# Third half of the attention: its queries and keys turned by DMA transposes in place of TensorE, weight loads put in another order, and one exponential placed later

## The chip, the cores and the metric

The kernel runs on one core of one Trainium2 chip. The metric is the device time of the whole kernel in microseconds; the time before is 238.54 us, the median of three runs (237.76 to 238.59). The trace is of one further execution, with a span of 236.1 us.

## The reference

An attention with a sliding window and a few global keys is followed by a feed-forward network with a ReLU gate. The attention takes 4 sequences of 768 positions, 8 heads of 64; each query sees 8 global keys and the last 96 keys, with a slope per head on the distance:

```python
keep = is_global | is_local
dist = np.where(is_global & ~is_local, float(n_local), np.abs(rel).astype(np.float32))
scores = scale * np.matmul(q, k.transpose(0, 1, 3, 2)) - slopes[:, None, None] * dist[None, :, :]
scores = np.where(keep, scores, -1000000000.0)
a = softmax(scores)
x = np.matmul(a, v)                     # -> 3072 tokens x 512
out = (np.maximum(x @ w_gate, 0.0) * (x @ w_val)) @ w_out   # 512 -> 1536 -> 512
```

## The kernel before

**Tiles and stages.** The 3072 tokens are cut into eight *halves* s = 0 to 7 of 384 query positions (half a sequence, all 8 heads). A half passes through three steps: queries and keys are loaded, cast to bf16 and transposed (features on partitions); attention gives xT, the transposed input of the feed-forward network; and the network gives 384 rows of output. Heads go in four pairs p = 0 to 3.

**Feed-forward.** For each of 12 chunks of the inner dimension there are two *items*, a gate and a value product, each of four matmuls of 128 x 384 (L745) and some 0.65 us. ScalarE takes the ReLU of the gate (L754) and VectorE multiplies it by the value product (L761). The output product works on pairs of 128 tokens and saves multiplications by sums of blocks: sums of w_out (`weight_sums`, L597, eight VectorE subtractions, once in the kernel: four matrices T, each in two parts for the two halves of the chunks), sums of the hidden values (L624 to L627), and seven products p1 to p7 (L631) whose partial results are copied by ScalarE (L660) and added by VectorE (L644). The weights come in three groups of four chunks (`wg[i]`, `wv[i]`), w_out in one tile `wo_sb`.

**Attention.** `attention_pieces(s)` is a list of 30 entries: units of scores (L512: matmuls into PSUM banks, of which one comes from `av_psum`, two banks, and the others from `qk_psum`, three banks), exponentials on ScalarE (L521), masks on VectorE (L533), value products `piece_av(s, p, e)` (L431, one for each head e of pair p, each in an `av_psum` bank), whose last lines are a logarithm of the row sums on ScalarE (L440) and, for the second head of the pair, exp(-log) (L445, the inverse), and `piece_norm` (L450), the products on VectorE of the value product and the inverse, which write xT and free the bank.

**What sets the order.** Everything is written out in one order, by `weave`: items of the feed-forward network of half c come one after the other, and pieces with a position between 0 and 1 are put in as soon as that share of the feed-forward work is done. `spread(items, first, last)` gives the i-th of n pieces the position first + (i + 0.5)/n times the stretch. The engines take their instructions in this order; an instruction whose input isn't ready holds up what is behind it on its engine. In the loop at L995 (c = 2 to 7) attention of half c + 1 lies beside the network of half c (`spread` from 0 to 0.87 for an even c, 0.85 for an odd one). The networks of halves 0 and 1 are woven together in two weaves (L985, L991), the first over weight groups 0 and 1, the second over group 2 and the output products, with attention of half 2 beside it.

**Transposes.** From half 3 on, `early_pieces(s)` does them: casts on GpSimd (L366), three transposing transfers for the keys and three for the queries, issued by SyncE (L371), and, again on GpSimd, copies that put the keys in order (L374). Half 2 does it in another way: GpSimd casts into `obuf` (L258 and L975), TensorE transposes by 24 small matmuls (L299, called by `T2_piece`), VectorE copies the keys (L278 to L280) and ScalarE the queries (L982).

**Loads.** GpSimd issues most transfers of this phase one after the other on one queue: weight groups 1 and 2 (L173), keys and queries of half 2 (L113), w_out (L923) and, after the casts of half 2, the values of half 2 (L162).

Of the kernel before, what the change touches and what calls it, by code (L numbers as in the profile page):

```python
# [8 lines left out]
FP32 = mybir.dt.float32  # L9
BF16 = mybir.dt.bfloat16  # L10
FP16 = mybir.dt.float16
AF = mybir.ActivationFunctionType
# [4 lines left out]
def kernel(  # L17
# [12 lines left out]
    nc = tc.nc  # L30
# [4 lines left out]
    DM = H * D  # L35
    DFF = moe_w_gate.shape[1]
    N_DC = DM // 128
    N_FC = DFF // 128
    HP = H // 2
    QH = S // 2  # L40
# [6 lines left out]
    scale = 1.0 / math.sqrt(D)  # L47
# [7 lines left out]
    for half in range(2):  # L55
# [14 lines left out]
    rc_pool = ctx.enter_context(tc.tile_pool(name="rc", bufs=2))  # L70
    xt_pool = ctx.enter_context(tc.tile_pool(name="xt", bufs=3))
# [19 lines left out]
    qT2 = [qTb[1].rearrange("d p e t -> d (p e t)")[:, i * HP * QH : (i + 1) * HP * QH].rearrange(  # L91
        "d (p t) -> d p t", p=HP) for i in range(2)]
# [9 lines left out]
    wo_sb = const.tile([128, N_FC, DM], FP16)  # L102
# [59 lines left out]
    def load_v_half(s):  # L162
        b, half = divmod(s, 2)
        if half == 0:
            load_v_globals(b)
            spread_v_globals(b)
        for j in range(4) if half == 0 else range(4, NT):
            load_v(b, j)

    def load_w(dst, src, f0, f1):  # L170
        nc.gpsimd.dma_start(out=dst, in_=src[:, f0:f1].rearrange("(c p) f -> p c f", p=128))  # L171

    def load_w_group(i):  # L173
        load_w(wg[i], moe_w_gate, i * GW * 128, (i + 1) * GW * 128)
        load_w(wv[i], moe_w_val, i * GW * 128, (i + 1) * GW * 128)

    for p in range(HP):
        load_qk(0, 2 * p, 2 * p + 2)
# [72 lines left out]
    QKB, FFB, AVB = (qk_psum, "qk_ps"), (ff_psum, "ff_ps"), (av_psum, "av_ps")  # L251
    xT_of = {}
# [35 lines left out]
    def piece_t(s, p, pool=av_psum, name="av_ps", apart=False):  # L288
        for i in (1, 0):
            if i == 1 or apart:  # L290
                tp = pool.tile([128, 512], FP32, name=name)
                tp = tp[:, 0:QH].bitcast(BF16).rearrange("d (i t) -> d i t", i=2)
            tp_of[s, p, i] = tp[:, i, :]
            for n in range(NN):
                for e in range(2 if s == 1 else 1):
                    r = slice(64 * e, 64 * e + 64) if s == 1 else slice(0, 128)
                    src = (qk16[s, i][:, 2 * p + e, n * D : (n + 1) * D] if s == 1
                           else cast_of[s, p][:, i, n])
                    nc.tensor.matmul(tp[r, i, n * 128 : (n + 1) * 128],  # L299
                                     lhsT=src, rhs=ident, is_transpose=True,  # L300
                                     start=((i == 1 or apart) and n == 0),
                                     stop=((i == 0 or apart) and n == NN - 1))

    def piece_copy_k(s, p):
        b, half = divmod(s, 2)
        put_keys(nc.vector.tensor_copy, nc.vector.tensor_copy, kT[b % 2][p], tp_of[s, p, 1], half)
# [71 lines left out]
    def early_pieces(s):  # L378
        out = [(0.0, lambda p=p: piece_cast2(s, p, kc, ks_of)) for p in range(HP)]
        out += [(0.0, lambda n=n: piece_x(kNb[s % 2], kc[s % 2], n)) for n in range(NN)]  # L380
        out += [(0.0, lambda p=p: piece_cast2(s, p, qc, qs_of)) for p in range(HP)]
        out += [(0.0, lambda n=n: piece_x(qT2[s % 2], qc[s % 2], n)) for n in range(NN)]
        out += [(0.0, lambda p=p: piece_order(s, p)) for p in range(HP)]
        return out
# [35 lines left out]
    def piece_av(s, p, e):  # L420
        b, half = divmod(s, 2)
        h = 2 * p + e
        vb = vbuf[b % 2]
        av = av_psum.tile([128, 512], FP32, name="av_ps")
        av_of[s, p, e] = av
        av3 = av[:, 0:QH].rearrange("d (n p) -> d n p", n=NN)
        todo = [t for bank in banks_of_half[half] for t in bank]
        for i, (j, a, w, m) in enumerate(todo):
            es, c = es_of[s, p, j, e]
            z0 = 2 * D * h + (D if e == 0 else 0)  # L430
            nc.tensor.matmul(av3[:, :, a : a + w],  # L431
                             lhsT=vb[:, j, z0 : z0 + 128],
                             rhs=es[:, c : c + NN * w].rearrange("k (n p) -> k n p", n=NN),
                             start=(i == 0), stop=(i == len(todo) - 1),
                             skip_group_check=True)
        o0, d0 = (0, 64) if e == 0 else (64, 0)
        if e == 0:
            av_of[s, p, "l"] = rc_pool.tile([128, QH], FP32, name="lnd")
        ln = av_of[s, p, "l"]
        nc.scalar.activation(ln[o0 : o0 + 64], av[d0 : d0 + 64, 0:QH], AF.Ln, bias=0.0, scale=1.0)  # L440
        if e == 1:
            if s not in xT_of:
                xT_of[s] = xt_pool.tile([128, N_DC, QH], BF16, name="xT")
            rc = rc_pool.tile([128, QH], FP32, name="rcp")
            nc.scalar.activation(rc, ln, AF.Exp, bias=0.0, scale=-1.0)  # L445
            av_of[s, p, "r"] = rc

    def piece_norm(s, p, e):
        r = slice(64 * e, 64 * e + 64)
        nc.vector.tensor_tensor(xT_of[s][r, p, :], av_of[s, p, e][r, 0:QH], av_of[s, p, "r"][r],  # L450
                                op=ALU.mult)
# [88 lines left out]
    def attention_pieces(s):  # L540
        masks, units = [], []

        def flush():
            for f in masks:
                f()
            masks.clear()

        def scores(groups, pools):
            units.extend(score_unit(s, groups, list(pools)))

        def x(scored=None):
            ready = masks[:]
            masks.clear()
            if scored:
                scores(*scored)
            masks.append(unit_exp(s, *units.pop(0)))
            for f in ready:
                f()

        U = [([(0, 0), (0, 1)], (AVB, QKB, QKB, QKB)),  # L560
             ([(0, 2), (1, 0)], (AVB, QKB, QKB, QKB)),
             ([(1, 1), (1, 2)], (AVB, QKB, QKB, QKB))]
        X = lambda u=None: [(0.0, lambda: x(u))]
        AV = lambda p: [(0.0, lambda e=e: (flush(), piece_av(s, p, e))) for e in range(2)]
        N = lambda p: [(0.0, lambda: (piece_norm(s, p, 0), piece_norm(s, p, 1)))]
        wait = [(0.0, lambda: None)]
        a0, a1 = AV(0), AV(1)

        return (X(U[0]) + X() + X() + X() + wait + X(U[1]) + X() + X() + a0[0:1] + X() + a0[1:2] + N(0) + wait
                + X(U[2]) + X() + a1[0:1] + X() + X() + a1[1:2] + N(1) + wait * 2 + AV(2) + N(2) + wait * 2  # L570
                + AV(3) + N(3))


    out_v = out.rearrange("(s p n) d -> s n p d", p=128, n=NN)
# [17 lines left out]
    def weight_sums(i0, i1):  # L592
        b = lambda f, d: B(i0, i1, f, d)
        t = lambda n: T(n, i0, i1)
        for out_, x, y in ((t(1), b(0, 1), b(0, 0)), (t(2), b(1, 1), t(1)),
                           (t(4), b(1, 0), t(2)), (t(3), b(1, 1), b(0, 1))):
            yield lambda o=out_, x=x, y=y: nc.vector.tensor_tensor(o, x, y, op=ALU.subtract)  # L597
# [207 lines left out]
    def spread(items, first, last):  # L805

        n = len(items)
        return [(first + (i + 0.5) / n * (last - first), f) for i, (_, f) in enumerate(items)]
# [14 lines left out]
    def cast(s, p, ek, eq):  # L823
        piece_cast(s, p, 1, ek)
        piece_cast(s, p, 0, eq)
# [11 lines left out]
    def AV(s, p, *pools):  # L837
        piece_av_wide(s, p, *pools)
        piece_norm_wide(s, p)
# [78 lines left out]
    piece_biased(1, 0)  # L918
    load_v(0, 3, 24)
    load_w_group(1)  # L920
    load_w_group(2)
    load_qk(2, 0, H, nc.gpsimd)
    load_w(wo_sb, moe_w_out, 0, DM)  # L923
    for f in gate[0:3]:
        f(0, LAST)
    for f in gate[0:3]:
# [45 lines left out]
    nc.gpsimd.memset(vbuf[1][:, NT - 1, :].bitcast(mybir.dt.uint32), 0)  # L972
    for j in range(NT):
        fill_ones(nc.gpsimd, 1, j)
    for p in range(HP):  # L975
        cast(2, p, P, P)
    load_v_half(2)

    def T2_piece(p):
        piece_t(2, p, *QKB, apart=True)  # L980
        piece_copy_k(2, p)
        nc.scalar.copy(qT2[0][:, p], tp_of[2, p, 0])  # L982

    T2 = [(0.0, lambda p=p: T2_piece(p)) for p in range(HP)]
    weave(f1_1[G[0]] + f1_0[G[1]][4:] + f1_1[G[1]],  # L985
          [(0.05 + 0.06 * j, lambda j=j: fill_ones(nc.vector, 0, j)) for j in range(NT)],
          [(0.1 + 0.2 * i, lambda h=h: setup_mask(h)) for i, h in enumerate((0, 1, 6, 7))],
          [(0.6, lambda: load_qk(3, 0, H)), (0.6, lambda: load_v_half(3))],
          spread(T2, 0.55, 0.95))
    sums_wo = [(0.0, f) for i in (0, 3) for f in weight_sums(i, i + 3)]  # L990
    weave(f1_0[G[2]] + f1_1[G[2]] + f2_0 + f2_1,  # L991
          spread(attention_pieces(2), 0.02, 0.86), spread(early_pieces(3), 0.1, 0.76),
          spread(sums_wo, 0.08, 0.4))

    for c in range(2, NHALF):  # L995
        placed = []
# [43 lines left out]
```

The softmax here doesn't subtract the row's maximum and nothing guards it: scores larger than these inputs give would overflow.

## Time and profile before

| | |
|---|---|
| time, median of 3 | 238.54 us (237.76 to 238.59) |
| span of the trace | 236.1 us |
| TensorE busy | 228.7 us, 97% of the span |
| VectorE busy | 186.9 us, 79% |
| ScalarE busy | 146.2 us, 62% |
| GpSimd busy | 89.0 us, 38% |
| moved by DMA | 30.43 MB, mean 129 GB/s |

The busy share of an engine is a mean over stages with different limits. The chain of waits goes back from the last instruction and says for each moment who held up the end: TensorE has 83% of it. The slices are 40 equal parts of the span, each digit a busy share in tenths. In the timelines a row gives start, duration, engine, line and what is done; what stands in brackets is the idle time before it and what ended that.

### The profile page before, as it was taken

What the parts mean: (1) busy time and instruction counts of PE and PEld (TensorE: products, weight loads), DVE (VectorE), ACT (ScalarE), POOL (GpSimd) and SP (SyncE); (2) the same over time, 40 slices, a digit from 0 to 9 for tenths busy, and PEclk for the clock granted to TensorE, in tenths of its full rate; (3) what the DMA queues carried; (4) which work ended last, traced back from release to release, by engine and by line L of the source; (5) the groups of instructions that cost most, each with busy time, mean ns of one, the idle gap of its engine ahead of it and who ended that gap; (6) DMA issues with size and microseconds to landing.
All of it is one profiled execution on the core that took longest, in us unless ns stands there. A gap on an engine that the chain in (4) does not pass through costs nothing.

```text
span 236.1 us, 5512 instructions
## 1 busy us (share of the span) xinstructions
PE 228.7 (97%) x2021; PEld 157.7 (67%) x2021; DVE 186.9 (79%) x466; ACT 146.2 (62%) x321; POOL 89.0 (38%) x191
## 2 busy tenths in 40 slices
PE   7898999999999999999999999999999999999994
PEld 3674766656678666856688566856688566865683
DVE  6876867879988779886999779876899779863784
ACT  7988865667624887467842787557742687624310
POOL 8997913933483066406580066405340000000000
PEclk9999999999999999999999999999999999999999
DMA  5999999998459856856397764846412200020005
GB/s 167 203 168 183 206 262 282 171 118 267 72 155 170 250 149 106 52 176 204 90 81 119 236 175 90 53 143 214 93 44 89 92 0 3 0 92 0 1 3 178
DMA packets 71419, 30.43 MB, mean 129 GB/s; under 512 B 47744, under 2 KB 70784, under 8 KB 71392
## 3 DMA queue, kind: packets, MB, share of 16 engines
q0 software_dynamic: 34896, 10.27, 38.7%
q1 hardware_dynamic: 36496, 19.82, 29.7%
q8 instruction: 16, 0.26, 0.5%
q14 instruction: 11, 0.09, 0.1%
HBM read 28.38 MB, written 6.29 MB: 147 GB/s over the span
## 4 chain that ended last, share of the span: by engine, by line
PE 83%; DVE 5%; POOL 4%; DMA 4%; ACT 2%; issue 1%; POOLq 0%; DVEq 0%
PE ff_ps L745 49%; PE ff_ps L631 19%; PE av_ps L431 6%; DMA kc<-in_q_dram 4%; PE ff_ps L778 2%; PE av_ps L512 2%; PE qk_ps L512 2%; POOL vbuf L154 1%; DVE wo_sum L597 1%; DVE obuf L644 1%; DVE ht L761 1%; DVE es L533 1%; POOL kc L131 1%; PE av_ps L465 1%; POOL wg L171 1%
## 5 line engine op out<-in xcount | busy, mean ns | idle before, releaser
L754 ACT ACTIVATE grelu<-ff_ps 128x384 bf16<-128x384 f32 x96 | 46.8, 489 | 52.6 <-PE ff_ps L745 39.3
L745 PE MATMUL ff_ps<-xT,wg 128*128 128x384 bf16 x384 | 77.9, 326 | 0.2 <-DMA wg<-in_moe_w_gate_dram 0.2
L745 PE MATMUL ff_ps<-xT,wv 128*128 128x384 bf16 x384 | 77.9, 326 | 0.0
L761 DVE TENSOR_TENSOR ht<-ff_ps,grelu 128x384 f16<-128x384 f32 x96 | 53.4, 557 | 27.6 <-PE ff_ps L745 23.5
L745 PEld LDWEIGHTS <-wv 128*128 128x128 bf16 x384 | 36.0, 98 | 23.9 <-issue 1.1
L745 PEld LDWEIGHTS <-wg 128*128 128x128 bf16 x384 | 36.3, 97 | 21.7 <-issue 0.7
L450 DVE TENSOR_TENSOR xT<-av_ps,rcp 64x384 bf16<-64x384 f32 x48 | 26.6, 553 | 6.1 <-ACT rcp L445 5.3
L367 POOL CAST kc<-ks 128x384 bf16<-128x384 f32 x20 | 10.6, 569 | 54.5 <-DMA ks<-in_k_dram 54.5
L644 DVE TENSOR_TENSOR obuf<-ff_ps,obuf 128x512 f32<-128x512 f32 (+1 forms) x46 | 27.6, 604 | 3.6 <-PE ff_ps L631 0.9
L440 ACT ACTIVATE lnd<-av_ps 64x384 f32<-64x384 f32 x48 | 23.3, 485 | 11.1 <-PE av_ps L431 10.2
L533 DVE TENSOR_TENSOR es<-es,m_all 128x432 bf16<-128x432 bf16 (+3 forms) x108 | 29.9, 321 | 0.2 <-ACT es L521 0.2
L521 ACT ACTIVATE es<-qk_ps 128x432 bf16<-128x432 f32 (+2 forms) x54 | 27.6, 531 | 0.0
L154 POOL DMA_DIRECT2D vbuf<-in_v_dram x29 | 24.7, 860 | 0.1
L431 PEld LDWEIGHTS <-vbuf 128*128 128x128 bf16 x216 | 18.2, 98 | 4.8 <-DVE xT L450 0.4
L431 PE MATMUL av_ps<-es,vbuf 128*128 128x216 bf16 (+4 forms) x216 | 21.4, 226 | 0.0
L631 PEld LDWEIGHTS <-ht 128*128 128x128 f16 x198 | 18.6, 97 | 3.5 <-issue 0.8
L631 PEld LDWEIGHTS <-hsum 128*128 128x128 f16 x192 | 18.5, 98 | 2.1
L631 PE MATMUL ff_ps<-wo_sb,ht 128*128 128x256 f16 x132 | 18.3, 272 | 0.0
L631 PE MATMUL ff_ps<-wo_sum,hsum 128*128 128x256 f16 x144 | 17.2, 272 | 0.0
L445 ACT ACTIVATE rcp<-lnd 128x384 f32<-128x384 f32 x24 | 12.6, 523 | 0.8
L521 ACT ACTIVATE es<-av_ps 128x432 bf16<-128x432 f32 (+2 forms) x18 | 9.5, 527 | 2.0 <-PE qk_ps L512 2.0
L512 PEld LDWEIGHTS <-kT 64*128 64x128 bf16 x216 | 6.6, 94 | 6.1 <-issue 3.8
(130 smaller groups left out, 263.6 us busy)
## 6 DMA issues: line engine op xcount, KB each, us to landing
out_dram<-obuf SPq DMA_DIRECT2D x22, 256.0 KB
ks<-in_k_dram SPq DMA_DIRECT2D x5, 768.0 KB
qs<-in_q_dram SPq DMA_DIRECT2D x5, 768.0 KB
vbuf<-in_v_dram POOLq DMA_DIRECT2D x23, 120.0 KB, 4.7
wv<-in_moe_w_val_dram POOLq DMA_DIRECT2D x3, 512.0 KB, 10.5
wo_sb<-in_moe_w_out_dram POOLq DMA_DIRECT2D x1, 1536.0 KB, 21.0
wg<-in_moe_w_gate_dram POOLq DMA_DIRECT2D x2, 512.0 KB, 10.3
ks<-in_k_dram SPq DMA_DIRECT2D x4, 192.0 KB
```

The source lines that it names most:

```text
L154: nc.gpsimd.dma_start(out=v_dst(b, NG + r0, NG + r0 + n, j), in_=v[b, :, KT * j + r0 : KT * j + r0 + n, :].rearrange("h p d -> p h d"))
L431: nc.tensor.matmul(av3[:, :, a : a + w], lhsT=vb[:, j, z0 : z0 + 128], rhs=es[:, c : c + NN * w].rearrange("k (n p) -> k n p", n=NN), star ...
L440: nc.scalar.activation(ln[o0 : o0 + 64], av[d0 : d0 + 64, 0:QH], AF.Ln, bias=0.0, scale=1.0)
L450: nc.vector.tensor_tensor(xT_of[s][r, p, :], av_of[s, p, e][r, 0:QH], av_of[s, p, "r"][r], op=ALU.mult)
L512: nc.tensor.matmul(banks[e][:, c : c + NN * w], lhsT=kT[b % 2][p][r, j, :], rhs=q3[:, :, a : a + w], start=True, stop=True)
L521: nc.scalar.activation(es[:, 0:cols], ps[:, 0:cols], AF.Exp, bias=0.0, scale=scale)
L533: nc.vector.tensor_mul(e4, e4, mk)
L631: nc.tensor.matmul(ps[:, c0 : c0 + DH], lhsT=lhs(i), rhs=rhs(i), start=(i == 0), stop=(i == NP - 1), skip_group_check=True)
L644: add = lambda o, x, y: nc.vector.tensor_tensor(o, x, y, op=ALU.add)
L745: nc.tensor.matmul(st[key][:, 0:QH], lhsT=w_of(w, dc, fc), rhs=xT_of[c][:, dc, :], start=(dc == 0), stop=(dc == N_DC - 1))
L754: nc.scalar.activation(gr, psg[:, 0:QH], AF.Relu, bias=0.0, scale=1.0)
L761: nc.vector.tensor_tensor(ht[:, fc, :], psv[:, 0:QH], st["r", fc], op=ALU.mult)
```

## The change

The keys and queries of half 2 are transposed as those of the later halves are, by `early_pieces(2)`, so that TensorE, VectorE and ScalarE have no part in it. The transfers are re-ordered for it: keys and queries of half 2 come before weight group 2, which GpSimd now issues behind its casts of half 2; w_out comes in two loads, one ahead of these casts and one behind. The copies that order the keys follow the loads of the values on GpSimd. With VectorE free of the key copies, half of the sums of w_out goes into the first weave (positions 0.6 to 0.95), the other half stays in the second (0.2 to 0.4); attention of half 2 is placed from 0.09 to 0.9 in place of 0.02 to 0.86. Last, the inverse of pair 3 is a piece of its own after the value product of its second head, in all halves from 2 on; the list has 31 entries by that.

```diff
+    def load_wo(i):
+        f = N_FC // 2
+        nc.gpsimd.dma_start(out=wo_sb[:, i * f : (i + 1) * f], in_=moe_w_out[
+            i * f * 128 : (i + 1) * f * 128].rearrange("(c p) f -> p c f", p=128))
...
-        if e == 1:
-            if s not in xT_of:
-                xT_of[s] = xt_pool.tile([128, N_DC, QH], BF16, name="xT")
-            rc = rc_pool.tile([128, QH], FP32, name="rcp")
-            nc.scalar.activation(rc, ln, AF.Exp, bias=0.0, scale=-1.0)
-            av_of[s, p, "r"] = rc
+        if e == 1 and p < HP - 1:
+            piece_inverse(s, p)
+
+    def piece_inverse(s, p):
+        rc = rc_pool.tile([128, QH], FP32, name="rcp")
+        nc.scalar.activation(rc, av_of[s, p, "l"], AF.Exp, bias=0.0, scale=-1.0)
+        av_of[s, p, "r"] = rc
...
-                + AV(3) + N(3))
+                + AV(3) + [(0.0, lambda: piece_inverse(s, 3))] + N(3))
...
     load_w_group(1)
-    load_w_group(2)
     load_qk(2, 0, H, nc.gpsimd)
-    load_w(wo_sb, moe_w_out, 0, DM)
+    load_wo(0)
...
-    for p in range(HP):
-        cast(2, p, P, P)
+    early = early_pieces(2)
+    for _, f in early[:-HP]:
+        f()
+    load_w_group(2)
+    load_wo(1)
     load_v_half(2)
...
-    T2 = [(0.0, lambda p=p: T2_piece(p)) for p in range(HP)]
+    for _, f in early[-HP:]:
+        f()
+
+    sums_wo = [[(0.0, f) for f in weight_sums(i, i + 3)] for i in (0, 3)]
...
-          spread(T2, 0.55, 0.95))
-    sums_wo = [(0.0, f) for i in (0, 3) for f in weight_sums(i, i + 3)]
+          spread(sums_wo[0], 0.6, 0.95))
     weave(f1_0[G[2]] + f1_1[G[2]] + f2_0 + f2_1,
-          spread(attention_pieces(2), 0.02, 0.86), spread(early_pieces(3), 0.1, 0.76),
-          spread(sums_wo, 0.08, 0.4))
+          spread(attention_pieces(2), 0.09, 0.9), spread(early_pieces(3), 0.1, 0.76),
+          spread(sums_wo[1], 0.2, 0.4))
```

More of the change, by code (lines that the diff above doesn't have):

```diff
@@ L440, in piece_av @@
         nc.scalar.activation(ln[o0 : o0 + 64], av[d0 : d0 + 64, 0:QH], AF.Ln, bias=0.0, scale=1.0)
-        if e == 1:
-            if s not in xT_of:
-                xT_of[s] = xt_pool.tile([128, N_DC, QH], BF16, name="xT")
-            rc = rc_pool.tile([128, QH], FP32, name="rcp")
-            nc.scalar.activation(rc, ln, AF.Exp, bias=0.0, scale=-1.0)
-            av_of[s, p, "r"] = rc
+        if e == 1 and p < HP - 1:
[4 more added lines that the diff above has]
+        av_of[s, p, "r"] = rc
     def piece_norm(s, p, e):
+        if s not in xT_of:
+            xT_of[s] = xt_pool.tile([128, N_DC, QH], BF16, name="xT")
         r = slice(64 * e, 64 * e + 64)
@@ L974 @@
         fill_ones(nc.gpsimd, 1, j)
-    for p in range(HP):
-        cast(2, p, P, P)
-    load_v_half(2)
[L979 to L982, printed above, removed]
-    T2 = [(0.0, lambda p=p: T2_piece(p)) for p in range(HP)]
+    early = early_pieces(2)
[3 more added lines that the diff above has]
+    load_wo(1)
+    load_v_half(2)
+    for _, f in early[-HP:]:
+        f()
+    sums_wo = [[(0.0, f) for f in weight_sums(i, i + 3)] for i in (0, 3)]
     weave(f1_1[G[0]] + f1_0[G[1]][4:] + f1_1[G[1]],
```

## The prediction

> **What bounds the kernel now.** I read the first page's busy times, the slices over the span, the chain of waits, then the timelines of the stages that the edits touch.
>
> ```profile
> PE 228.7 (97%) x2021; PEld 157.7 (67%) x2021; DVE 186.9 (79%) x466; ACT 146.2 (62%) x321; POOL 89.0 (38%) x191
> PE   7898999999999999999999999999999999999994
> DVE  6876867879988779886999779876899779863784
> DMA  5999999998459856856397764846412200020005
> PE 83%; DVE 5%; POOL 4%; DMA 4%; ACT 2%; issue 1%; POOLq 0%; DVEq 0%
> ```
>
> TensorE is busy from about 25 us to the end and is 83% of the chain, so work taken off it counts fully, and any wait put in front of it counts too. DMA is full up to 53 us. The chain shows where something else holds TensorE: VectorE around 50 to 59 us, and later ScalarE for a moment.
>
> ```profile
> 40.54 0.34 PE qk_ps L299 x6
> 42.17 0.34 PE qk_ps L299 x6
> 58.81 0.47 DVE xT L450
> 59.33 0.26 PE av_ps L512
> 124.69 0.49 ACT lnd L440
> 125.20 0.52 ACT rcp L445
> 125.73 0.27 ACT obuf L660
> 126.04 1.03 PE ff_ps L631 x8
> ```
>
> (Columns: start, duration, what.) The L299 groups are the third half's transposes. At 59.33 a score group waited for an attention output (L450). At 126.04 a product waited for a ScalarE copy (L660) that stood behind a logarithm and an exponential.
>
> ```profile
> 50.00:55.00 5.00, 5.00 (x43) 2.96 (x42) 4.63 (x13) 3.91 (x10) 0.00 (x0) 1.00 1.15 117
> 55.00:60.00 5.00, 4.85 (x41) 2.96 (x40) 4.94 (x12) 3.58 (x9) 2.97 (x5) 1.00 0.76 259
> 83.00:88.00 5.00, 5.00 (x47) 3.13 (x46) 3.74 (x10) 4.14 (x10) 3.83 (x8) 1.00 0.48 139
> ```
>
> (Stretch and length; busy time of TensorE, its weight loads, VectorE, ScalarE, GpSimd; clock; DMA share; GB/s.) VectorE is full from 50 to 60 us, where the eight weight sums (L597, 0.3 to 0.85 us each) lie. At 83 to 88 us, a steady stage, it is not.
>
> **What the Trainium skill says.** "TensorE: Matmul & The Clock Gate", section "Wait — 56ns, not 53.3ns?": a warm matmul follows the last after its columns at 2.4 GHz and about 2.5 ns; 24 transposes of 128 columns are then 24 x 55.8 = 1.34 us, and the trace agrees (four groups at 0.34). "DMA: Bandwidth & Descriptors", section "Queues, rings and completion order": a DMA engine serves the queues that have work in turn, packet by packet. So transposes and weight loads in flight together share the engines; before, the two never met while TensorE waited, so no run here shows it.
>
> **The change, part by part.**
>
> *Transposes.* Four TensorE groups go: 4 x 0.34 = **-1.34 us**, on the path. Twelve VectorE key copies (L278 to L280, 1.1 us for each pair of heads) go from 40 to 47 us, and four ScalarE copies (L982, 0.48 us); nobody waited for these there, so they count nothing.
>
> *Weight sums.* Half of the eight go to the time that the key copies leave free. VectorE is relieved by about 2 us between 50 and 59, and the wait at 59.33 (TensorE idle 58.85 to 59.33 of which 0.15 is the gap of any score group) goes: **-0.25 us** (estimate 0.2 to 0.4).
>
> *Loads.* Now keys and queries of the third half follow the second weight group, at the pitch of the landings in the trace: wv1 at 35.7 stood behind wg2, which in turn moves. In place of ks landing 37.65 and qs 39.62, ks lands near 32.5 and qs near 34.5, and the first half of wo near 38.3. GpSimd (waiting 7.48 us for ks before the cast at 37.70, see below) starts the casts at 32.6; eight at about 0.46 us and the wait for qs end at 36.4. Only then do the issues of wg2, wv2 and wo's second half come, 0.8 us each; then the values' loads. Uncontended, at 2.55 us for each half megabyte, wg2 lands near 40.9, wv2 43.4, the second wo 47.2, the values' globals 47.4. The deadlines: gate 8 reads wg2 at 46.91 now, at 45.6 with the transposes gone; val 8 reads wv2 at 46.2; the second sums read wo at about 52; the values are read at 54.6. There are 4.7 and 2.8 us of slack.
>
> ```profile
> 37.70 0.50 POOL L263 CAST obuf<-ks 128x384 bf16<-128x384 f32 x1 [7.48 <-DMA ks<-in_k_dram]
> 59.65 3.92 SPq L372 DMA_TRANSPOSE kN<-kc  x3
> ```
>
> Against this stand the six DMA transposes, from 34.5 to 42.3 by the pitch of the next half (3.92 us for three), in the same stretch. How much of the engines they take there is not shown. Lower bound 0 (the engines fit them between the packets of the loads). Upper bound: a burst of all engines of 0.65 us each, as the next half's seem to be, all pushed in front: 6 x 0.65 = 3.9 us, wg2 at 44.8, wv2 at 47.3, i.e. a wait of 47.3 - 46.2 = 1.1 us, and later values another 0.4. I take 0, because the slack covers 2.8 of the 3.9 us. The key copies on GpSimd now stand behind the value loads' issues (43 to 47.4); the first scores at 48.3 - 1.3 = 47.0 want the first pair at about 44. Small risk, 0.
>
> *The last exponential.* Its inverse of pair 3 becomes an item of its own behind the second value product. In stages c=3 and c=5 the copy L660 is then ahead of it: the waits at 126.04 (0.23) and 179.75 (0.23) go: **-0.46 us**. An attention output at 146.28 (0.17) profits too: **-0.17 us**.
>
> But the list of attention pieces has 31 in place of 30 items, and `spread` gives position (i+0.5)/31 of the same stretch: *all* pieces of all later stages move forward by up to 3%, that is by none or one feed-forward item of 0.65 us. In stages c=2, 4 and 6 the order of instructions changes from [value product, 2 items, value product, 3 items, scores, 1 item] to [.., 2 items, .., 2 items, scores, 2 items]: the third score unit comes one item earlier.
>
> ```profile
> 83.90 0.47 PE L431 MATMUL av_ps<-es,vbuf 128*128 128x72 bf16 x5
> 84.21 0.81 PE L745 MATMUL ff_ps<-xT,wg 128*128 128x384 bf16 x4
> 84.85 0.81 PE L745 MATMUL ff_ps<-xT,wv 128*128 128x384 bf16 x4
> 85.50 0.81 PE L745 MATMUL ff_ps<-xT,wg 128*128 128x384 bf16 x4
> 86.25 0.25 PE L512 MATMUL av_ps<-qT,kT 64*128 64x192 bf16 x1
> ...
> 85.50 1.14 DVE L450 TENSOR_TENSOR xT<-av_ps,rcp 64x384 bf16<-64x384 f32 x2
> ```
>
> (The last line is VectorE's timeline.) The unit at 86.25 needs an av_ps bank of two; it is freed by the first of the two products L450, 85.50 to 86.07. That one waits for logarithm and exponential (84.42 to 85.46) of the value product at 83.90, which doesn't move. One item earlier the unit would start at 85.6 and cannot before 86.2: TensorE idles about **0.5 us**, and the feed-forward item that hid it now comes after. The products L450 of pair 2 similarly: the first value product of pair 3 (95.79) moves one item forward to 95.14, but its bank is freed by a product that stands behind a ReGLU product and a sum on VectorE until 94.75, so it ends at 95.4 or so: **0.38 us**. The pair before: 0.12 us. Together 1.0 us a stage, three stages: **+3.0 us**. Bounds: 0.4 a stage if only the first is real and partly covered, 1.2 if the delays push ScalarE and VectorE work behind. I take 1.0. In stages c=3 and 5, I find value products an item earlier and no bank missing: 0.
>
> *Placement 0.09 to 0.9.* In the second weave the attention starts 7% of the stretch later; it gives the loads some slack and is otherwise neutral: 0.
>
> Sum: -1.34 - 0.25 - 0.46 - 0.17 + 3.0 = **+0.8 us**; 238.54 + 0.8 = 239.3.
>
> **Rivals.**
> *A, the moved items find room.* The stalls of the even stages are half as long, because a wait early in the stage makes the later ones shorter (TensorE's wait at the third unit also gives VectorE time for pair 2). Then +1.0 instead of +3.0: 238.5 - 1.2 = 237.3; with 0 it is 236.3. For it: VectorE has idle gaps around 84 and 88. Against: both waits are chains of fixed length from a value product that moves with TensorE. 0.27.
> *B, the loads are late (slower).* The transposes displace the weights fully: +1.1 for wv2, +0.4 for the values, on top of the main case: 240.8. For it: the DMA share of the slices is 9 until 53 us, and wg2 is issued 14 us later than now. Against: 2.8 us slack. 0.22.
> *C, stalls gone and loads late:* about 238.5. 0.06.
>
> **How the numbers follow.** Main case 0.45 at 239.3 (238.5 to 240.2, about a third of it above 239.73), A 0.27 at 237.0 (236.3 to 237.8, two thirds below 237.35), B 0.22 at 240.8, C 0.06. Faster by over 0.5% (below 237.35): from A, 0.2. Slower (above 239.73): 0.15 of the main case and all of B, 0.37. The rest, 0.43, within 0.5%. The range takes in A's middle and most of B: 236.8 to 241.2.
>
> **What would show it.** After: no L299 groups between 40 and 46; no wait of the gate and value products of weight group 2 (L745's idle column for a weight load stays near 0.2); the score group near 59 without a VectorE wait; in the three even stages, gaps of about 0.5 us before the third score unit that the chain gives to the attention output product; none before product p4 at 126 and 180. If the even stages keep their length, A is right. If TensorE idles at 45 to 48 us for a weight, B is. The prediction is wrong if the stalls shift other engines' queues into a better order, which static positions don't show.

## The result and the profile after

The changed kernel takes 248.34 us (median of 6 runs, 247.36 to 249.12) where the kernel before takes 237.95 us (236.97 to 238.59): a ratio of 1.044, 95% interval 1.040 to 1.048. Forecast were 239.3 us and a range of 236.8 to 241.2. The line numbers below are those of each kernel's own text; in the changed one the items are L753 (before L745), the scores L520 (L512), the value products L436 (L431), `piece_norm` L458 (L450), and the transposes L377 (L372). Where executions of one kernel lie more than 1.5% apart, as with x7 and x12 below, the ratio is taken from the faster ones.

The first page of the changed kernel, the lines that answer to those shown of before:

```profile
PE 231.2 (94%) x1997; PEld 157.8 (64%) x1997; DVE 187.6 (76%) x454; ACT 145.5 (59%) x317; POOL 94.8 (38%) x204
PE   5889999939899999999999999999999999999994
DVE  5688867614999778977799877977799876964684
PEclk9799999967999999999999999999999999999999
DMA  6999999999329893369439584568330400020004
PE 69%; DMA 12%; DVE 9%; ACT 5%; SPq 1%; issue 1%; POOL 0%; DVEq 0%; ACTq 0%
```

TensorE has a hole in the ninth slice (49 to 55 us) that was not there, and in it and behind it the clock is at 6 and 7 tenths. Of the chain of waits DMA now has 12%, against 4%. Half of that is the first load of w_out, on the chain from 24.6 to 38.5 us, where TensorE was busy all the time; the rest is what it waited for:

```profile
38.91 1.30 SPq L377
40.25 1.33 SPq L377
41.63 11.82 DMA qT<-qc
53.59 0.34 PE av_ps L520
54.10 0.39 PE qk_ps L520 x5
54.49 5.30 PE ff_ps L753 x20
```

The last query transpose was issued at 41.63 and had landed at 53.45; the first scores of half 2 waited for it, with TensorE idle for 4.08 us. The stretches around it, in the columns used before (TensorE, its weight loads, VectorE, ScalarE, GpSimd, clock, DMA share, GB/s):

```profile
49.00:51.00 2.00, 0.51 (x4) 0.10 (x1) 0.56 (x1) 0.39 (x1) 2.00 (x6) 1.00 1.35 179
51.00:53.00 2.00, 0.00 (x0) 0.00 (x0) 0.00 (x0) 0.00 (x0) 1.27 (x2) 0.64 1.97 149
55.00:57.00 2.00, 2.00 (x8) 0.95 (x7) 0.09 (x1) 1.08 (x3) 0.00 (x0) 0.50 2.30 150
57.00:59.00 2.00, 2.00 (x10) 1.04 (x9) 1.14 (x3) 0.78 (x3) 0.00 (x0) 0.65 0.89 179
```

From 49.5 to 53.6 TensorE has nothing; from 51.6 to 58.4 its clock is half, and from 54.4 to 58.2 the matmuls of an item start 0.32 us apart in place of 0.16.

Where the 10 us arose is seen best by setting the start of the same feed-forward item in two traces side by side. There are 192 items, 24 for each half; the number is what the difference to the trace of before grew by in the stretch:

| stretch | after | 31 pieces, rest as before (x2) |
|---|---|---|
| up to item 8 (start of the kernel) | +1.3 | -0.8 |
| items 8 to 32 (both groups, transposes of half 2 among them) | -1.4 | +0.9 |
| items 32 to 40 (first scores of half 2) | +5.9 | 0.0 |
| item 40 to the start of c=2 (rest of the second weave) | +1.7 | -0.2 |
| c=2 | +1.25 | +1.5 |
| c=3 | -0.3 | -0.3 |
| c=4 | +1.0 | +1.0 |
| c=5 | -0.3 | -0.2 |
| c=6 | +1.0 | +1.0 |
| sum | +10.1 | +2.9 |

The start of the kernel is the same code in all and differs by -0.8 to +1.3 among the profiled executions (a first load of queries that lands a us sooner or later); I count it as no effect. What x2 gained there it gave back by item 24, in a wait.

### The profile page after: what moved, and what is told of

Its sections match the earlier page's. It is cut to its first block, busy times and chain, and to the rows that moved or that the text cites. A ratio compares the mean times of both kernels' runs of the same rounds, so it can differ in the third digit from the quotient of the medians.

```text
span 246.4 us, 5459 instructions
## 1 busy us (share of the span) xinstructions
PE 231.2 (94%) x1997; PEld 157.8 (64%) x1997; DVE 187.6 (76%) x454; ACT 145.5 (59%) x317; POOL 94.8 (38%) x204
## 3 DMA queue, kind: packets, MB, share of 16 engines
q0 software_dynamic: 34912, 10.27, 38.1%
## 4 chain that ended last, share of the span: by engine, by line
PE 69%; DMA 12%; DVE 9%; ACT 5%; SPq 1%; issue 1%; POOL 0%; DVEq 0%; ACTq 0%
PE ff_ps L753 37%; PE ff_ps L639 19%; DMA wo_sb<-in_moe_w_out_dram 6%; PE av_ps L436 5%; DMA qT<-qc 5%; PE av_ps L520 2%; PE ff_ps L786 2%; DVE ht L769 2%; PE qk_ps L520 2%; DMA qs<-in_q_dram 2%; DVE xT L458 1%; SPq L377 1%; ACT grelu L762 1%; DVE obuf L652 1%; DVE es L541 1%
## 5 line engine op out<-in xcount | busy, mean ns | idle before, releaser
L762 ACT ACTIVATE grelu<-ff_ps 128x384 bf16<-128x384 f32 x96 | 46.8, 491 | 56.3 <-PE ff_ps L753 40.0
L753 PE MATMUL ff_ps<-xT,wg 128*128 128x384 bf16 x384 | 79.1, 330 | 0.2
L753 PE MATMUL ff_ps<-xT,wv 128*128 128x384 bf16 x384 | 78.6, 328 | 0.0
L753 PEld LDWEIGHTS <-wg 128*128 128x128 bf16 x384 | 37.0, 98 | 23.8 <-issue 2.9
L753 PEld LDWEIGHTS <-wv 128*128 128x128 bf16 x384 | 36.3, 98 | 23.8 <-issue 1.7
L541 DVE TENSOR_TENSOR es<-es,m_all 128x432 bf16<-128x432 bf16 (+3 forms) x108 | 33.5, 354 | 4.5 <-ACT es L529 4.5
L372 POOL CAST kc<-ks 128x384 bf16<-128x384 f32 x24 | 12.7, 573 | 62.6 <-DMA ks<-in_k_dram 62.6
L458 DVE TENSOR_TENSOR xT<-av_ps,rcp 64x384 bf16<-64x384 f32 x48 | 26.6, 554 | 5.7 <-ACT rcp L451 4.8
L436 PEld LDWEIGHTS <-vbuf 128*128 128x128 bf16 x216 | 17.8, 98 | 7.1 <-DVE xT L458 2.9
L436 PE MATMUL av_ps<-es,vbuf 128*128 128x216 bf16 (+4 forms) x216 | 21.5, 226 | 0.6 <-DVE xT L458 0.5
L520 PEld LDWEIGHTS <-kT 64*128 64x128 bf16 x216 | 6.8, 95 | 12.2 <-issue 7.9
## 6 DMA issues: line engine op xcount, KB each, us to landing
wv<-in_moe_w_val_dram POOLq DMA_DIRECT2D x3, 512.0 KB, 10.1
```

The costliest lines, as they stand in the source:

```text
L436: nc.tensor.matmul(av3[:, :, a : a + w], lhsT=vb[:, j, z0 : z0 + 128], rhs=es[:, c : c + NN * w].rearrange("k (n p) -> k n p", n=NN), star ...
L520: nc.tensor.matmul(banks[e][:, c : c + NN * w], lhsT=kT[b % 2][p][r, j, :], rhs=q3[:, :, a : a + w], start=True, stop=True)
L541: nc.vector.tensor_mul(e4, e4, mk)
L753: nc.tensor.matmul(st[key][:, 0:QH], lhsT=w_of(w, dc, fc), rhs=xT_of[c][:, dc, :], start=(dc == 0), stop=(dc == N_DC - 1))
L762: nc.scalar.activation(gr, psg[:, 0:QH], AF.Relu, bias=0.0, scale=1.0)
```

## The experiments

**The piece list.** The last edit undone in the changed kernel, and alone in the kernel before:

```diff
# x1_thirty_pieces, against after
-        if e == 1 and p < HP - 1:
+        if e == 1:
...
-                + AV(3) + [(0.0, lambda: piece_inverse(s, 3))] + N(3))
+                + AV(3) + N(3))
# x2_inverse_only: before, with the same lines as in after
```

> The changed kernel with the last edit undone: the inverse of pair 3 is again computed with the second value product, so the attention list has 30 pieces. Theory (two causes: the transfers' delay early on, and the shift of the pieces, which costs about 1.1 us in each of the stages c=2, 4, 6 and gains 0.3 in c=3 and 5): 248.3 - 3.3 + 0.6 = 245.6 us, the stages c=2 to 6 as long as before the change. Rival (all of the loss is from the early wait for the transposed queries; the later differences are its after-effects): 248.3 us.

> The kernel before with the last edit alone, the separate inverse of pair 3 and so 31 pieces. Theory (shift of pieces): 238.0 + 3.3 - 0.6 = 240.7 us, c=2, 4, 6 each about 1.1 us longer and c=3, 5 each 0.3 shorter. Rival (the later stages only pass on a delay of the early ones): 238.0 us or a little less.

Measured: x1 244.89 us (ratio to before 1.028, 1.024 to 1.032), x2 240.99 us (1.013, 1.010 to 1.016; before beside them 237.89). In x1 no stretch from c=2 on differs from before by more than 0.2 us. In x2 the stages with an odd half cost 1.5, 1.0 and 1.0 us, the others gain 0.2 to 0.3, with all transfers as before. So the shift of the pieces is a cause of its own, about 3 us net. In each of the three stages some 0.5 us of it arises at the third score unit, in x2 and in the changed kernel alike. The wait itself, in x2's timeline of TensorE and then of VectorE:

```profile
84.71 0.81 PE L748 MATMUL ff_ps<-xT,wv 128*128 128x384 bf16 x4
85.96 0.25 PE L515 MATMUL av_ps<-qT,kT 64*128 64x192 bf16 x1 [0.43 <-DVE xT L453]
...
85.35 1.14 DVE L453 TENSOR_TENSOR xT<-av_ps,rcp 64x384 bf16<-64x384 f32 x2 [0.38 <-ACT rcp L446]
```

Before, three items of 0.65 us stood between the value product and this unit and the bank was free in time; now two do, and the unit waits for the first of the two products that free the bank.

**Only where it pays.** The kernel before, with the separate inverse in the halves 2, 4 and 6 alone:

```diff
# x6_inverse_even, against x2
-        if e == 1 and p < HP - 1:
+        if e == 1 and (p < HP - 1 or s % 2 == 1):
...
-[(0.0, lambda: piece_inverse(s, 3))]
+([(0.0, lambda: piece_inverse(s, 3))] if s % 2 == 0 else [])
```

> The kernel before with the separate inverse of pair 3 only in the halves 2, 4 and 6, whose attention lies in the second weave and in c=3 and c=5; the odd halves keep 30 pieces. Theory (the extra piece costs 1.1 us in each stage with an odd half and saves 0.2 to 0.3 in each with an even one): 238.0 - 0.2 - 0.3 - 0.2 = 237.2 us, c=2, 4, 6 unchanged. Rival (the gains in c=3 and 5 only give back part of what the stage before lost): 238.0 us.

Measured: 237.00 us, before beside it 237.53: ratio 0.9971 (0.9959 to 0.9984). The stretches of c=3 and c=5 gain 0.31 us each, c=2, 4 and 6 change by 0.2 or less. This is a small gain, 0.5 us, but the one version here that beats both kernels.

**Transposes back on TensorE.** The changed kernel with `T2_piece` again (casts, copies and spread 0.55 to 0.95 as before), all other edits kept:

```diff
# x3_tensor_transposes, against after
-    early = early_pieces(2)
-    for _, f in early[:-HP]:
-        f()
+    for p in range(HP):
+        cast(2, p, P, P)
     load_w_group(2)
     load_wo(1)
     load_v_half(2)
-    for _, f in early[-HP:]:
-        f()
+    T2 = [(0.0, lambda p=p: T2_piece(p)) for p in range(HP)]
...
-          spread(sums_wo[0], 0.6, 0.95))
+          spread(sums_wo[0], 0.6, 0.95), spread(T2, 0.55, 0.95))
```

> The changed kernel, but half 2 transposed on TensorE as before, with loads, sums and placement as changed. Theory (the transposing transfers share the DMA engines with the loads and come too late; slow clock and a late VectorE in the second weave follow from that wait): the gap of 4.2 us, the slow matmuls (1.9) and most of the 1.7 us lost in the output products of the second weave go, the transposes come back: 248.3 - 5.9 - 1.7 + 1.3 = 242.0 us. Rival (the weight loads are late or the placement 0.09 to 0.9 with its sums is what costs): weave two stays long, 244 us or more.

Measured: 241.16 us (1.014, 1.011 to 1.016). The hole is gone and the clock is 1.00 from 45 to 60 us, so the half clock came with the hole. The transposing transfers, with all that follows from them, thus cost some 7 us here (248.34 against 241.16). Against x2, which has the 31 pieces too, there is 0.2 us left for new loads, sums and placement together, less than single executions differ by.

**Which transfer gives way.** Three runs change what is in flight beside the transposes.

```diff
# x5_transposes_alone, against after: nothing beside them (sums of w_out all in the second weave,
# load_wo(0) taken out of its earlier place, key copies ahead of the loads)
     early = early_pieces(2)
-    for _, f in early[:-HP]:
+    for _, f in early:
         f()
+    seen = const.tile([128, 8], BF16)
+    nc.gpsimd.tensor_copy(seen, qT2[0][:, 0, QH - 8 : QH])
+    load_wo(0)
     load_w_group(2)
# x4b_loads_behind, against after: w_out's second half and the values later
     load_w_group(2)
-    load_wo(1)
-    load_v_half(2)
     for _, f in early[-HP:]:
         f()
+    load_wo(1)
+    load_v_half(2)
# x11_half_packets, against after: the same bytes in packets of half the size
-    load_w_group(2)
-    load_wo(1)
+    for dst, src in ((wg[2], moe_w_gate), (wv[2], moe_w_val)):
+        for f in (0, 256):
+            load_w(dst[:, :, f : f + 256], src, 2 * GW * 128 + f, 2 * GW * 128 + f + 256)
+    for d in (0, 256):
+        nc.gpsimd.dma_start(out=wo_sb[:, 6:12, d : d + 256], in_=moe_w_out[
+            768:1536, d : d + 256].rearrange("(c p) f -> p c f", p=128))
```

> The disputed cost by itself: the changed kernel, but weight group 2, all of w_out and the values of half 2 are issued by GpSimd only when it has read the last transposed query, so no load is in flight beside the six transposes; the sums of w_out all lie in the second weave. The time is of no interest, since gate 8 now waits for its weights. Theory (sharing): three key transposes are through about 4.5 us after the first issue, all six after 8 to 9 us, as in half 3, against 11.6 and 18.7 us in the changed kernel. Rival (slow by themselves, or SyncE's queue): again above 15 us.

> The changed kernel, transposes by transfers, but w_out's second half and the values of half 2 are issued behind the ordering of the keys, so that fewer loads share the engines with the transposes. Theory (packets of loads and transposes take turns, so less load means earlier transposes): queries land near 48.5 in place of 53.5 us, the wait for them shrinks to 0.5 us or less, no slow clock, 248.3 - 5.9 = 242.4 us if the values are in time. Rival (the transposes are slow by themselves, held by their issue on SyncE): queries land near 53 us again and the time stays at 248.

> The changed kernel with weight group 2 and w_out's second half each loaded in two column halves, so that their packets are 512 bytes in place of 1024 and twice as many, the bytes the same. Theory (weight and transposing packets take turns one for one): a pair takes less time, so transposing packets come at clearly more than the 153 in a us seen beside 1024-byte packets, the queries land 2 us or more earlier than 53.5 and the wait ahead of the first scores shrinks from 4.2 to 2 us or so; the weights land later in return. Rival (bytes are shared, or transposes wait for the loads' queue to drain): the queries land at 53 us or later.

In x5 GpSimd reads the first key and the last query at

```profile
40.67 0.53 POOL L283 COPY kT<-kN 128x360 bf16<-128x360 bf16 x1 [3.06 <-DMA kN<-kc]
44.51 0.19 POOL L985 COPY seen<-qT 128x8 bf16<-128x8 bf16 x1 [0.61 <-DMA qT<-qc]
```

that is 5.3 and 9.1 us after the first issue at 35.41, where the changed kernel takes 11.7 and 18.6 us (34.83 to 46.49 and 53.45). By themselves the six are not slow. (The time of x5, 256.08 us in one execution, says nothing: its products wait for their weights.) The packets of the two queues (q0 carries GpSimd's loads, q1 SyncE's transposes) from 42 to 50 us in the changed kernel, then from 44 to 47.5 us in x11, then x5's transposes from 36 to 45 us:

```profile
q0 software_dynamic: 1246, 1.25, 92.6%
q1 hardware_dynamic: 1224, 0.30, 29.0%
```

```profile
q0 software_dynamic: 868, 0.43, 88.6%
q1 hardware_dynamic: 872, 0.22, 47.0%
```

```profile
q1 hardware_dynamic: 3264, 0.79, 38.9%
```

(Packets, MB, share of 16 engines.) As many packets of the one as of the other, to 2%: in these stretches the queues take turns in equal numbers. A packet of a weight load has 1024 bytes and one of a transpose 256, so beside such a load the transposes get a fifth of the bytes, 0.30 MB in 8 us; alone they would need 1.3 us for that by x5's row (0.79 MB in 38.9% of 9 us, that is 3.5 us). With 512-byte packets the turns come round faster, 249 in a us in place of 153. x11 took 241.97 us in one execution, before 237.38 beside it; the clock stayed at 1.00, and two waits are left, the first for the last query (landed at 48.6) and a key copy that ends with it, the second for the global values:

```profile
48.72 0.25 PE L520 MATMUL av_ps<-qT,kT 64*128 64x216 bf16 x1 [0.98 <-POOL kT L285]
57.42 0.59 PE L436 MATMUL av_ps<-es,vbuf 128*128 128x216 bf16 x3 [2.18 <-DMA vbuf<-vbuf]
```

The faster turns are shown by this; that the whole 6 us between after and x11 come from them is not. In x11's one trace the first keys landed a us sooner, in the start of the kernel that the edit leaves alone, while the weight loads were issued no sooner. The first issues of transposes and loads in the changed kernel, and then in x11, with the transposing packets up to 39.5 us behind each:

```profile
34.83 3.92 SPq L377 DMA_TRANSPOSE kN<-kc  x3
36.67 0.77 POOL L171 DMA_DIRECT2D wg<-in_moe_w_gate_dram  x1
q1 hardware_dynamic: 1067, 0.26, 60.3%
```

```profile
33.72 3.91 SPq L377 DMA_TRANSPOSE kN<-kc  x3
36.70 1.52 POOL L171 DMA_DIRECT2D wg<-in_moe_w_gate_dram  x2
q1 hardware_dynamic: 1600, 0.39, 70.3%
```

A transpose is 544 packets (3264 for six), so two were through before the loads in the changed kernel and three in x11; the others had to share. The three that were left in x11 took 7.2 us, 2.4 each. With a fourth of the same length the queries would have landed near 51 (an estimate), and some half of the 4.9 us gained at this point is the head start.

x4b: 250.25 us (1.051, 1.046 to 1.055), slower still, yet the last transposing packets went at 47.1 (52.5 in the changed kernel), the last query landed at 47.7, and the scores started at 48.59 without a wait. The wait went to the values, whose issues stood behind the key copies on GpSimd, and these behind the key transposes:

```profile
58.58 0.25 PE L436 MATMUL av_ps<-es,vbuf 128*128 128x216 bf16 x1 [3.56 <-DMA vbuf<-in_v_dram]
63.03 0.60 PE L436 MATMUL av_ps<-es,vbuf 128*128 128x216 bf16 x3 [4.20 <-DMA vbuf<-vbuf]
```

So the expectation for the queries held (47.7 for 48.5), that for the time didn't. (A first form, x4, has no time: it put sums of w_out behind products that read them.)

**Two attempts to have the transposes for nothing.** x7 gives them only weight group 2 beside them; values and all of w_out come behind the key copies:

```diff
# x7_transposes_first, against after (and load_wo(0) ahead of the casts taken out, all sums of w_out
# at 0.3 to 0.5, attention of half 2 at 0.04 to 0.87, the separate inverse in even halves only)
     load_w_group(2)
-    load_wo(1)
-    load_v_half(2)
     for _, f in early[-HP:]:
         f()
+    load_v_half(2)
+    load_wo(0)
+    load_wo(1)
# x12_half_packets_best, against after (and the second sums of w_out at 0.3 to 0.42, the separate
# inverse in even halves only)
+    load_v_globals(1)
     early = early_pieces(2)
     for _, f in early[:-HP]:
         f()
-    load_w_group(2)
-    load_wo(1)
-    load_v_half(2)
+    for dst, src in ((wg[2], moe_w_gate), (wv[2], moe_w_val)):
+        for f in (0, 256):
+            load_w(dst[:, :, f : f + 256], src, 2 * GW * 128 + f, 2 * GW * 128 + f + 256)
+    spread_v_globals(1)
+    for j in range(3):
+        load_v(1, j)
     for _, f in early[-HP:]:
         f()
+    load_v(1, 3)
+    load_wo(1)
```

> Transposes of half 2 by transfers with only weight group 2 beside them: the order on GpSimd is casts, weight group 2, key ordering, values, then both loads of w_out; all sums of w_out in the second weave at 0.3 to 0.5, attention of half 2 at 0.04 to 0.87, separate inverse in the even halves only. Theory (turns packet by packet, 0.1 us for a pair of a weight and a transposing packet on each engine): queries land at about 47, no wait over 0.5 us for them, no slow clock; if values and w_out are in time 238.0 - 1.3 - 0.7 = 236.0 us, with VectorE or w_out late by up to 2 us 238.0. Rival (transposes beside any load are too late): a gap of 2 us or more ahead of the first scores of half 2, over 240 us.

> An attempt at a kernel that beats both: the changed kernel with weight group 2 in column halves (512-byte packets), the global values of half 2 loaded ahead of its casts and spread behind the transposes, three of its value loads ahead of the key ordering and the fourth and w_out's second half (one load) behind it, the second sums of w_out at 0.3 to 0.42, and the separate inverse in even halves only. Theory (turns packet by packet; small value packets beside the query transposes): no wait of more than 1 us for transposes, weights or values, no slow clock: x11's 242.0 - 3.3 (odd halves) - 2.3 (wait for the spread globals) - about 1 (key ordering earlier) = 235.4 us. Rival (the transfers of this phase are too much for the time up to the first scores, and a wait only moves): 237.5 us or more, no better than before.

Measured: x7 245.88 to 251.62 us in six executions (1.041, 1.037 to 1.046), x12 240.64 to 244.90 us in six (1.020, 1.016 to 1.024); the trace is of the slowest execution of each. The longest wait of TensorE in x7, and then the two of x12 at the scores and the output products:

```profile
67.07 0.26 PE L520 MATMUL av_ps<-qT,kT 64*128 64x216 bf16 x1 [4.64 <-DVE xT L458]
```

```profile
49.15 0.25 PE L520 MATMUL av_ps<-qT,kT 64*128 64x216 bf16 x1 [1.47 <-DMA qT<-qc]
63.18 1.44 PE L786 MATMUL ff_ps<-wo_sb,ht 128*128 128x512 f16 x3 [4.45 <-DVE ht L769]
```

In x7 the last transposing packets went at 47.7, not far from the 47 expected, and the scores waited 0.2 us. But the value products waited 3.0 us in three parts for the values, and w_out landed at 64.7 and 70.6: VectorE, 5.9 us idle for it, came late with the sums and with all that stood behind them. In x12 the scores waited 1.5 us and the output products 4.5 us for VectorE, which stood at a sum of w_out's second half: issued 10 us later than in the changed kernel, and 14.0 us on its way beside the loads of half 3, which SyncE could now issue at 47.6 in place of 56.3, it landed at 62.1 in place of 51.1. This is what the rival of x12 says: in these orders a wait only moves. That no order would do is not shown.

**The rest of the second weave.**

```diff
# x8_placement_back, against x3
-          spread(attention_pieces(2), 0.09, 0.9), ...
+          spread(attention_pieces(2), 0.02, 0.86), ...
# x9_placement_before, against x2
-          spread(attention_pieces(2), 0.02, 0.86), ...
+          spread(attention_pieces(2), 0.09, 0.9), ...
# x10_sums_back, against x3
-          spread(sums_wo[0], 0.6, 0.95), spread(T2, 0.55, 0.95))
+          spread(T2, 0.55, 0.95))
...
-          spread(sums_wo[1], 0.2, 0.4))
+          spread(sums_wo[0] + sums_wo[1], 0.08, 0.4))
```

> x3_tensor_transposes with the attention of half 2 placed at 0.02 to 0.86 again (sums of w_out, loads and 31 pieces as changed). Theory (the 1.1 us lost between the output products and the next stage in x3 is from the later placement, which puts attention's masks and products on VectorE beside the sums of hidden values): 241.2 - 1.1 = 240.1 us. Rival (the sums of w_out, four in 0.2 to 0.4, are what VectorE is late with): 241.2 us.

> x2_inverse_only with the attention of half 2 placed at 0.09 to 0.9 as in the change; loads, transposes and sums as before. It asks where the 1.1 to 1.7 us go that the second weave (between the last items of weight group 2 and the start of c=2) is longer by. Theory (the later placement puts masks and products on VectorE beside the sums of hidden values): 1 us or more in that stretch, 242 us. Rival (loads of half 3 and the split sums): within 0.3 us of x2_inverse_only, 241 us.

> x3_tensor_transposes with all eight sums of w_out in the second weave at 0.08 to 0.4 as before; loads and placement 0.09 to 0.9 as changed. Theory (placement): the second weave stays 1 us or more longer than before the change. Rival (the split sums, four of them at 0.2 to 0.4): the loss goes, 240 us.

Measured: x8 242.13 us (1.019, 1.016 to 1.021), x9 240.56 and x10 241.64 (one execution each, before 237.38). Neither of the two named causes holds. From item 32 to the start of c=2, which takes in the pieces that the placement moves over item 40, x9 differs from before by 0.0 us, x3 by +0.55, x10 by +0.5. x9 and x10 differ in the order of the loads alone (w_out in two among it), so half a us seems to belong to that, on one trace each. x8 adds a wait of 0.9 us for the spread values, which the later placement hides. What the changed kernel loses in this stretch beyond wait and slow clock is some 1.5 us. Of these, TensorE stands 0.42 us before an output product at 66.15 and 0.42 us before the scores at 67.38, both for VectorE, which is busy for 4.90 of 5 us from 65 to 70; which of the sums, masks and late casts it is stays open.

## Why the prediction was wrong

**The step that failed** is the sharing of the DMA engines: "How much of the engines they take there is not shown. Lower bound 0 ... Upper bound: a burst of all engines of 0.65 us each ... all pushed in front ... I take 0, because the slack covers 2.8 of the 3.9 us." Both bounds ask how much the loads lose to the transposes. That was fairly right: wg2 and wv2 landed at 42.5 and 46.1, between the two bounds, no product of group 2 waited for them, and w_out's second half came at 51.1, 3.9 us after the 47.2 forecast for it undisturbed. Neither bound asks what the transposes lose to the loads. They were put at their pitch in half 3, where little else is in flight: from 34.5 to 42.3, with the first scores at 47.0. The last landed at 53.45, and TensorE stood idle for 4.08 us. Since its clock fell to half in that wait, another 1.9 us (12 matmuls at 0.32 in place of 0.16 us) came on top, which no case of the prediction had.

The delay has two parts. In x5, alone, the third transpose begins 3.9 us after the first issue and the last packet of the sixth goes 8.5 us after it; in the changed kernel these are 7.1 and 17.7 us. So 3.2 us are lost before the third begins, in a stall that is not explained (see "What stays open"), and some 6 us in the turns that follow. For the second part a sentence of the Trainium skill was quoted, "DMA: Bandwidth & Descriptors", section "Queues, rings and completion order": engines serve queues in turn, packet by packet. The trace agrees as far as numbers go (1246 and 1224 packets; the order of single turns isn't shown). With packets of 256 bytes beside 1024 it says that the small packets' queue is the one that is slowed. Both sizes stood in the trace of before: in order, transposes of half 3 (59.6 to 63.6 us) and the load of w_out (26 to 32 us).

```profile
q1 hardware_dynamic: 1102, 0.27, 29.6%
q0 software_dynamic: 1237, 1.23, 123.3%
```

**Transposes**, -1.34 us: right, items 8 to 32 gain 1.4 us in the changed kernel and 1.0 to 1.4 in the others that have the edit, x5 apart.

**The last exponential**: the two sides were right in mechanism and size. Forecast +3.0 us for c=2, 4, 6; measured +3.3 in the changed kernel and +3.6 in x2. The 0.5 us at the third score unit came as forecast; the rest was not followed wait by wait. Forecast -0.46 for c=3 and 5; measured -0.6 in the changed kernel and in x6. The 0.17 at 146.28 was none of it: x1 and x6, which leave the pieces of that stage as before, don't show the gap either, so it belongs to the one execution that was profiled. x2 alone would have been forecast at 238.5 + 2.4 = 240.9; that it measured 240.99 is in part luck, as its difference to before beside it is 3.1 us and not 2.4.

**Weight sums**, -0.25 us: wrong. The gain was read too large to begin with: the wait at 59.33, counted from 58.85, is 0.15 us by its row in the timeline. In the changed kernel everything behind comes later, and the score group waits for L458 at 67.38 again, for 0.42 us; x9, with the sums as before, does no worse than x3.

**Key copies on GpSimd**, "small risk, 0": wrong by its premise. They started at 46.49, not at 43, as they wait for the key transposes. In the changed kernel the query transposes come later still and hide it; in x4b and x7 loads are queued behind these copies on GpSimd, and the waits for values and w_out there are longer than the one for the queries was in the changed kernel (7.8 us in x4b).

**Placement**, 0: right as far as x9 shows it (0.0 us up to the start of c=2, one trace).

**Rivals.** B (loads late, 240.8) named the right place and the wrong victim. A (pieces find room) is refuted by x2, and C, which needs A's stalls to go, with it.

**What stays open.** The third key transpose of the changed kernel, issued at 37.48, waits while the first load of weight group 2 runs. From 39.5 to 41.5 us the two queues have

```profile
q0 software_dynamic: 361, 0.37, 117.6%
q1 hardware_dynamic: 21, 0.00, 1.4%
```

and no data packet of a transpose is among the 21. It begins at 41.9, when that load's last packets go (it lands at 42.5), 2.9 us after the load set in at 39.0. In x11 it is the first query transpose that waits so, from 39.2 to 40.9, and in x12 the third key transpose, from 38.1 to 39.7: 1.7 and 1.6 us, where the first load is half as long. Why the queues don't take turns in this time isn't shown. How much of x11's time is owed to the smaller packets, and how much to its earlier keys and the shorter stall, isn't either.

## What to carry to other kernels

When a transfer moves into a stretch where others are in flight, ask for both sides what they lose, and take the packets' sizes for it: two queues here moved equal numbers of packets, so the transfer of small packets was the one that came late, and cutting the rows of the load in two raised its turns from 153 to 249 in a us. Moving the loads behind it only moved the wait. A position that is a share of a list moves every piece when the list gets one longer: before adding a piece, look at which of the moved ones take a buffer that is only just free. And a wait of TensorE can cost more than its length: 4.1 us here brought 1.9 us of slow matmuls.

## What the runs showed of the hardware

- Queue turns: 153 packets in a us each for 1024-byte loads and 256-byte transposes, 249 each with 512-byte loads; transposes alone, 3264 packets in 3.5 us of the engines' time. A transpose that met the start of a load of 1024-byte packets had no turn in the first 2.9 us of it.
- TensorE's clock, in five traces:

| run | TensorE idle | clock at half |
|---|---|---|
| after | 49.51 to 53.59 (4.08 us) | 51.6 to 58.4 |
| x4b | 55.02 to 58.58 and 58.83 to 63.03 (3.56 and 4.20 us) | 59.4 to 66.3 |
| x12 | 58.73 to 63.18 (4.45 us) | 63.0 to 69.9 |
| x7 | 62.43 to 67.07 (4.64 us) | 67.5 to 70.9 |
| x11 | 0.98 and 2.18 us | not |

The fall came 2.1 to 5.1 us after the idle time began, and the stretches at half clock last 3.4 us or twice that.
